# RG-LRU scan and gated causal convolution: the last root batch multiplied in channel order, and a new order of all queues

## The chip, the cores and the metric

The kernel runs on one core of a Trainium2 chip. Its engines work side by side, each through its own list of instructions in order: PE (matrix products and transposes, with the weight loads shown apart as PEld), DVE (VectorE), ACT (ScalarE), POOL (GpSimd) and SP, which here only issues the DMAs. The metric is the device time of one execution in microseconds. Before the change it is 291.31 us, the median of three runs (291.29, 291.31, 292.64).

## The reference

For inputs x, r_gate and i_gate of shape (4, 6336, 256), in float32, a gated linear recurrence runs over the 6336 steps of each of the four sequences, for 256 channels:

```python
log_a = c * sig_r * np.log(np.clip(a_base, 1e-06, 1.0 - 1e-06))[None, None, :]
a_t = np.exp(log_a)
norm = np.sqrt(np.maximum(1.0 - a_t * a_t, 1e-06))
x_gated = norm * sig_i * x
for t in range(S):
    h = a_t[:, t] * h + x_gated[:, t]
```

Here sig_r and sig_i are the sigmoids of the two gates and c is 8. The states h then go through a small network: a causal convolution of 5 taps per channel and a sigmoid give a gate, `h @ w_val` gives a value, and the output is `(gate * value) @ w_out`.

## The kernel before

The 25344 rows are cut into 51 windows: windows 0, 1 and 50 of 256 rows, all others of 512. One window or two make a chunk (28 chunks): chunks 0, 1 and 2 are windows 0, 1 and 2, chunks 3 to 25 have two windows each (chunk 25 is windows 47 and 48), and chunks 26 and 27 are windows 49 and 50. A window is loaded with rows on the 128 partitions; the recurrence needs channels there, in two halves h of 128 channels. So data is turned by transposes on PE, which write to PSUM (eight banks).

The steps have short names, and the number behind a name is a window or a chunk (and a half):

- `lr`, `li`, `lx` (SP, L279): loads of r_gate, i_gate and x for a window, into rings of four places each. `st` (SP, L507): store of the output, from a ring of four.
- `ta`, `tb` (ACT, L297, L300): tanh of half of r and i, the sigmoids in another form, for a chunk. The results are bfloat16; `tb` writes a ring of four places.
- `tr` (PE, L344) transposes `ta`'s result, `ex` (ACT, L360) takes the exponential: the coefficient a_t, channels on partitions, for a half of one chunk or of a pair of chunks.
- `sq` (POOL, L368) squares a_t into `ering`, for a chunk and half; `sa` (ACT, L376) does the same on ACT.
- `rt` (ACT, L393): the norm's square root of all the chunks of a root batch. There are eight batches, since root and exponential need different tables on ACT and each change costs a table load (L523). The last batch, `rt.7.0`, is chunks 25, 26 and 27.
- `pp` and `up` (POOL, L307, L319): gate of i plus one, and times x, into `uring`, with two rows interleaved as pairs of bfloat16 that pass through PE as one float32 word. For a few windows `xp` (PE, L324) and `uv` (DVE, L333) do this instead, with x copied to PSUM by a product with the identity.
- `nt` (PE, L407) transposes the norm back to rows on partitions, `xg` (DVE, L414) multiplies it into `uring`, in place.
- `xt` (PE, L422) transposes the product to channels, one bank for each half, and `sc` (DVE, L444) scans it together with a_t: this is the recurrence, with states in `yring`.
- `cv` (PE, L456): the convolution, 20 products of 64 by 64 weights for a window. `tg` (ACT, L463): its gate, a tanh. `vl` (PE, L471): the value. `gv` (DVE, L476): gate times value. `ou` (PE, L486): the output product. `cd` (DVE, L494) or `ca` (ACT, L496): the copy of it from PSUM for the store.

Nothing schedules these at run time. A string, ORDER, lists every step once, and the kernel emits them in that order (L518 to L524), so each engine's list is ORDER cut down to its own steps. What stands behind an @ are the banks of PSUM. An instruction that has to wait, for data, for a bank or for a place in a ring, holds up everything behind it on its engine.

## Time and profile before

| | |
|---|---|
| median of three runs | 291.31 us |
| the profiled execution | 293.39 us |
| span of the profile, first to last instruction | 291.6 us |
| mean granted clock of TensorE | 0.981 |
| read from HBM, written to HBM | 78.39 MB, 25.95 MB |

The profile is that of one execution. A row of groups tells line, engine, operation, the tiles written and read, the shapes, the count, and behind the bar the busy time in us, the mean of one instruction in ns, and the idle time of the engine just before, with what ended it. A row of the timeline has the start and the length in us in front; neighbours of one kind are merged (x2 is two instructions), and in brackets stands the idle time ahead of it.

### The profile page before, as it was taken

To read this page: it belongs to the slowest core of one execution; us is meant where nothing else is said; L and a number is where in the kernel's file an instruction comes from. 1 tells how busy PE (TensorE), PEld (TensorE's weight loads), DVE (VectorE), ACT (ScalarE), POOL (GpSimd) and SP (SyncE) were. 2 spreads that over 40 slices of the span, in tenths; PEclk is the share of its full clock that TensorE was granted. 3 is DMA by queue.
4 is the path that set the end of the run, shared out by engine and by line. 5 is a ranking of instruction groups with operands and counts; after the bars stand their busy time and mean duration, and the time that the engine had idled before them with its cause. 6 is when DMAs were issued, how large, how long until landed. Compare 5 with 4: busy or idle time off the path is not lost. (4 is left out here: it accounts for less than half of the span.)

```text
span 291.6 us, 6228 instructions
## 1 busy us (share of the span) xinstructions
PE 244.7 (84%) x2482; PEld 168.5 (58%) x2507; DVE 243.5 (83%) x201; ACT 272.4 (93%) x191; POOL 235.2 (81%) x156
## 2 busy tenths in 40 slices
...
GB/s 239 316 386 405 383 407 385 380 371 333 395 411 418 416 415 366 285 418 416 418 416 416 411 411 416 419 388 378 416 416 420 415 326 276 267 288 110 290 87 239
DMA packets 29995, 104.75 MB, mean 359 GB/s; under 512 B 3335, under 2 KB 3854, under 8 KB 29966
## 3 DMA queue, kind: packets, MB, share of 16 engines
...
q14 instruction: 10, 0.08, 0.1%
q10 hardware_dynamic: 14, 0.01, 0.0%
HBM read 78.39 MB, written 25.95 MB: 358 GB/s over the span
## 5 line engine op out<-in xcount | busy, mean ns | idle before, releaser
L444 DVE TENSOR_TENSOR_SCAN yring<-aring,yring,banks 128x1024 bf16<-128x1024 f32 (+5 forms) x54 | 106.8, 1993 | 2.6 <-PE banks L422 1.3
L368 POOL TENSOR_TENSOR ering<-aring 128x1024 f32<-128x1024 f32 (+2 forms) x55 | 92.6, 1709 | 16.4 <-ACT aring L360 16.3
L319 POOL TENSOR_TENSOR uring<-tbring,xring 128x1024 bf16<-128x1024 bf16 (+1 forms) x45 | 95.3, 2136 | 1.5 <-DMA xring<-in_x_dram 0.8
L476 DVE SCALAR_TENSOR_TENSOR tgring<-tgring,banks 128x1024 bf16<-128x1024 bf16 (+1 forms) x51 | 59.3, 1181 | 7.8 <-PE banks L471 2.8
L456 PE MATMUL banks<-yring,diag 64*64 64x512 bf16 (+7 forms) x1080 | 63.2, 365 | 1.4 <-DVE tgring L476 0.4
L307 POOL TENSOR_SCALAR tbring<-tbring 128x1024 bf16<-128x1024 bf16 (+1 forms) x45 | 46.2, 1039 | 14.9 <-ACT tbring L300 14.8
L486 PE MATMUL banks<-wo,tgring 128*128 128x256 bf16 x396 | 50.5, 273 | 8.9 <-DVE tgring L476 6.2
L463 ACT ACTIVATE tgring<-banks 128x1024 bf16<-128x1024 f32 (+1 forms) x51 | 50.2, 1007 | 4.2 <-PE banks L456 4.1
L360 ACT ACTIVATE aring<-banks,khf 128x2048 f32<-128x2048 bf16 (+3 forms) x34 | 53.4, 1610 | 0.7 <-POOL ering L368 0.3
L471 PE MATMUL banks<-yring,wv 128*128 128x512 bf16 (+7 forms) x191 | 48.4, 359 | 4.9 <-ACT aring L360 1.6
L486 PEld LDWEIGHTS <-tgring 128*128 128x128 bf16 x396 | 42.3, 114 | 17.5 <-DVE tgring L476 7.6
L297 ACT ACTIVATE taring<-rring 128x2048 bf16<-128x2048 f32 (+2 forms) x28 | 47.7, 1722 | 1.9 <-DMA rring<-in_r_gate_dram 1.9
L300 ACT ACTIVATE tbring<-iring 128x2048 bf16<-128x2048 f32 (+2 forms) x28 | 48.0, 1727 | 0.3 <-DVE uring L333 0.3
L456 PEld LDWEIGHTS <-diag 64*64 64x64 bf16 x1080 | 30.3, 107 | 25.2 <-issue 9.7
L393 ACT ACTIVATE ering<-ering 128x2048 bf16<-128x2048 f32 (+4 forms) x11 | 44.1, 4042 | 0.1
L344 PE MATMUL banks<-ident_b,taring 128*128 128x128 bf16 x396 | 29.9, 230 | 12.0 <-ACT taring L297 8.3
L494 DVE COPY oring<-banks 128x1024 f32<-128x1024 f32 (+1 forms) x31 | 36.3, 1182 | 3.6 <-PE banks L486 3.5
L422 PE MATMUL banks<-ident,uring 128*128 128x128 f32 x198 | 30.8, 283 | 7.8 <-DVE uring L414 4.4
L344 PEld LDWEIGHTS <-taring 128*128 128x128 bf16 x396 | 25.5, 103 | 17.6 <-ACT taring L297 10.2
L471 PEld LDWEIGHTS <-wv 128*128 128x128 bf16 x216 | 19.5, 97 | 23.4 <-issue 10.0
L414 DVE TENSOR_TENSOR uring<-banks,uring 128x2048 bf16<-128x2048 bf16 (+2 forms) x28 | 30.2, 1092 | 2.5 <-PE banks L407 2.1
L422 PEld LDWEIGHTS banks<-ident,uring 128*128 128x128 f32 x198 | 22.0, 142 | 16.3 <-DVE uring L414 7.6
...
## 6 DMA issues: line engine op xcount, KB each, us to landing
...
```

Of the source, the lines that this page charges most:

```text
L300: nc.scalar.activation(**tangent(c, tbring, NTI, iring, NII))
L319: nc.gpsimd.tensor_tensor(out=u, in0=t1, in1=xt, op=ALU.mult)
L344: nc.tensor.transpose(out=bank[:, o:o + P], in_=taring[:, place(w, NTR), j, h * P:(h + 1) * P], identity=ident_b[:])
L360: nc.scalar.activation(out=dst, in_=src, func=ACT.Exp, scale=khf[:, h:h + 1], bias=khf[:, h:h + 1])
L368: nc.gpsimd.tensor_tensor(out=e, in0=a, in1=a, op=ALU.mult)
L422: nc.tensor.transpose(out=bank[:, o + q:o + wins[w] // 2:nq], in_=uring[:, (w + 1) % NU, q, h * P:(h + 1) * P, :].rearrange("p d two -> p ...
L444: nc.vector.tensor_tensor_scan(out=yring[:, h, col:col + o1 - o0], data0=aring[:, h, a_at[c] + o0:a_at[c] + o1], data1=xT[:, o0:o1], initi ...
L456: nc.tensor.matmul(out=gp[oh * 64:oh * 64 + 64, h, a:b], lhsT=diag[half * 64:half * 64 + 64, h, k, :], rhs=yring[half * 64:half * 64 + 64, ...
L463: nc.scalar.activation(out=tgring[:, w % NTG, :, 0:wins[w]], in_=live.pop(("gp", w))[:, :, 0:wins[w]], func=ACT.Tanh, scale=0.5)
L471: nc.tensor.matmul(out=val[:, m, a:b], lhsT=wv[:, hk, m * P:(m + 1) * P], rhs=yring[:, hk, col:col + b - a], start=(hk == 0), stop=(hk == ...
L476: nc.vector.scalar_tensor_tensor(out=tgring[:, w % NTG, :, 0:wins[w]], in0=tgring[:, w % NTG, :, 0:wins[w]], scalar=1.0, in1=live.pop(("va ...
L486: nc.tensor.matmul(out=ops[:, j * D:(j + 1) * D], lhsT=gv[:, hk, j:wins[w]:J], rhs=wo[:, hk, :], start=(hk == 0), stop=(hk == H - 1))
```

## The change

The change has two parts.

First, chunks from 25 on (DIRECT), which are the last root batch, take another way to the scan. Before: root, `nt` (norm to rows), `xg` (product in rows, in place), `xt` (product to channels, in PSUM), `sc`. Now the gated input is transposed alone, both halves into one stretch of banks, and it does not wait for the root; `xg` multiplies it, read from PSUM, with the norm as it lies in `ering`, in channel order, and writes the product to `uring`; and `sc` reads its second operand there, in SBUF, where all other chunks read PSUM. `nt` is gone for these three chunks.

Second, ORDER is new from end to end. The counts of steps that differ: `nt` 28 to 25; windows gated by `xp` and `uv` 0, 1, 2, 8, 9, 18 to 1, 2, 7, 9, and so by `pp` and `up` 45 to 47; `sq` 55 to 53 and `sa` 1 to 3 (chunk 14's half 0 and chunk 27's half 1 move to ACT); copies `cd` 31 to 33 and `ca` 20 to 18. The start and the end of the two orders, and the code:

```diff
+DIRECT = 25
...
 ORDER = """
-s_ident s_small s_kt s_diag lr.0 lr.2 lr.1 li.0 lr.3 ta.0 ta.2 lr.4 tr.0.1@5 ta.1 tr.2.0@4 ex.0.1 lr.5 tr.1.1@0
-tr.2.1@7 ex.2.0 lr.6 sq.0.1 ex.1.1 li.2 ex.2.1 tr.0.0@0 tb.0 tr.1.0@7 ex.1.0 li.4 ex.0.0 lx.1 sq.1.0 ta.3 s_wl.3 sq.2.0
-lx.0 li.3 sq.0.0 lx.3 ta.4 sq.1.1 li.1 sq.2.1 lx.2 lr.8 tb.2 tr.3.1@0,1 ex.3.1 tr.3.0@6,7 li.6 lr.9 xp.0@3 lr.7 uv.0
-lx.4 ex.3.0 sq.3.1 s_wl.0 s_wl.2 tb.3 sq.4.1 lr.10 tb.1 xp.2@4,5 sq.3.0 xp.1@0 s_wl.1 uv.1 rt.0.0 li.8 sq.4.0 li.5 pp.3
-nt.0@6 rt.1.0 nt.1@7 lx.6 xg.1 pp.4 xg.0 xt.0.1@2 sc.0.1 up.3 uv.2 xt.1.1@2 xt.1.0@3 nt.2@6 xg.2 up.4 lx.7 sc.1.1 lx.5
-xt.2.0@7 ta.5 xt.0.0@0 xt.2.1@6 li.7 sc.0.0 nt.3@4,5 sc.1.0 s_wcast ta.6 xg.3 lr.11 cv.0@2,3 lr.12 sc.2.1 cv.1@4,5 tg.0
...
+s_ident s_small s_kt s_diag lr.0 lr.2 lr.1 lr.3 li.0 ta.0 ta.2 lr.4 ta.1 lr.6 tr.2.1@4 tr.0.1@0 lr.5 ex.2.1 tr.0.0@2
+tr.2.0@5 li.2 ex.0.1 lx.0 ex.2.0 tr.1.0@0 li.1 tr.1.1@3 tb.0 s_wl.0 ex.0.0 lx.1 pp.0 ex.1.0 li.3 ex.1.1 li.4 ta.3
+sq.1.1 sq.2.1 lx.2 sq.0.0 ta.4 lr.8 sq.2.0 s_wl.2 up.0 lr.7 tb.2 tr.3.1@2,3 lx.3 sq.1.0 lx.4 ex.3.1 sq.0.1 tr.3.0@6,7
+lr.9 tb.1 sq.4.1 s_wl.1 ex.3.0 li.6 sq.3.1 tb.3 xp.1@7 sq.3.0 li.7 uv.1 lr.10 rt.0.0 sq.4.0 xp.2@4,5 lx.6 uv.2 s_wl.3
+pp.4 nt.0@2 li.5 rt.1.0 xg.0 lx.5 pp.3 xt.0.0@7 xt.0.1@6 nt.2@1 li.8 xg.2 up.3 sc.0.1 xt.2.1@3 sc.0.0 nt.1@6 xt.2.0@0
+xg.1 up.4 lx.7 xt.1.1@1 xt.1.0@5 cv.0@6,7 sc.1.0 ta.5 sc.2.0 nt.3@4,5 tg.0 sc.1.1 s_wcast lr.11 ta.6 lr.12 xg.3
...
-tb.25 xg.24 xt.23.1@2 ou.40.0@6,7 sc.23.1 tg.41 pp.47 ou.39.0@0,1 ca.40.0 xt.24.0@5 sq.25.0 xt.24.1@4 ca.39.0 st.40
-tr.26.0@7 sc.24.0 lx.47 ex.26.0 vl.41@2,3 lx.50 cv.42@0,1 sa.26.1 st.39 sq.26.0 tb.27 st.38 cv.43@6,7 gv.41 tg.42
-sq.27.0 pp.49 sc.24.1 cv.44@2,3 tg.43 pp.48 pp.50 vl.42@0,1 up.48 gv.42 rt.7.0 ou.41.0@6,7 vl.43@4,5 cd.41.0 up.47
-ou.42.0@0,1 gv.43 st.41 cv.45@6,7 cd.42.0 up.49 nt.25@4,5 tg.45 xg.25 vl.45@0,1 tg.44 vl.44@6,7 gv.45 up.50 xt.25.1@5
-gv.44 ou.43.0@2,3 ca.43.0 ou.45.0@0,1 sc.25.1 xt.25.0@4 ca.45.0 st.43 ou.44.0@2,3 st.45 cv.46@6,7 ca.44.0 st.42 sc.25.0
-st.44 tg.46 vl.46@0,1 nt.26@2 nt.27@5 xg.26 cv.47@6,7 xg.27 gv.46 xt.26.1@5 tg.47 xt.26.0@4 sc.26.1 vl.47@2,3
-ou.46.0@0,1 sc.26.0 xt.27.1@5 ca.46.0 cv.48@6,7 gv.47 st.46 cv.49@0,1 tg.48 sc.27.1 tg.49 vl.48@2,3 xt.27.0@7 gv.48
-ou.47.0@4,5 ca.47.0 sc.27.0 vl.49@0,1 gv.49 st.47 ou.48.0@2,3 cv.50@4,5 ca.48.0 tg.50 ou.49.0@6,7 st.48 ca.49.0
-vl.50@2,3 gv.50 st.49 ou.50.0@4 ca.50.0 st.50
...
+tb.25 gv.41 vl.39@2,3 tr.25.0@7 xt.23.1@6 gv.39 ex.25.0 tr.26.0@1 pp.48 ou.40.0@4,5 sc.23.1 ex.26.0 pp.47 ou.39.0@2,3
+ca.40.0 xt.24.1@0 sq.25.0 xt.24.0@1 ca.39.0 st.40 cv.42@4,5 sc.24.0 tb.27 st.39 sq.26.0 sa.27.1 cv.43@6,7 lx.50 tg.42
+up.47 sc.24.1 tg.43 vl.43@2,3 ou.41.0@4,5 up.48 vl.42@6,7 cd.41.0 rt.7.0 cv.45@0,1 gv.43 st.41 pp.49 xt.25@4,5 gv.42
+cv.44@2,3 up.49 xg.25 ou.42.0@6,7 tg.44 sc.25.0 pp.50 vl.45@4,5 tg.45 up.50 ou.43.0@2,3 ca.42.0 cv.46@0,1 gv.45 ca.43.0
+st.42 sc.25.1 tg.46 vl.44@6,7 st.43 ou.45.0@2,3 xt.26@4 ca.45.0 xt.27@5 gv.44 cv.48@0,1 st.45 xg.26 cv.47@2,3 tg.48
+xg.27 sc.26.0 ou.44.0@4,5 sc.26.1 tg.47 vl.46@0,1 ca.44.0 gv.46 vl.48@6,7 vl.47@2,3 st.44 sc.27.1 gv.48 ou.46.0@0,1
+cv.49@4,5 ca.46.0 gv.47 st.46 tg.49 ou.48.0@6,7 sc.27.0 ca.48.0 vl.49@0,1 gv.49 st.48 ou.47.0@4,5 cv.50@2,3 cd.47.0
+tg.50 ou.49.0@6,7 st.47 ca.49.0 vl.50@0,1 gv.50 st.49 ou.50.0@3 ca.50.0 st.50
 """
...
         def op_xg(c):
+            u = u_of(c)
+            if c < DIRECT:
+                nc.vector.tensor_tensor(out=u, in0=live.pop(("nT", c)).bitcast(BF16), in1=u, op=ALU.mult)
+                return
+
+            o = 2 * live["n", c]
+            nc.vector.tensor_tensor(out=u, in0=live.pop(("uT", c)).bitcast(BF16),
+                                    in1=ering[:].bitcast(BF16)[:, o:o + H * clen[c]], op=ALU.mult)
+            for h in range(H):
+                live["xT", c, h] = u[:, h * clen[c]:(h + 1) * clen[c]]
...
+        def op_xt(c, *at):
+
+            if c < DIRECT:
+                h, b = at
+                words(c, h, banks[:, b])
+                live["xT", c, h] = banks[:, b].bitcast(BF16)
+                return
+            ps = banks[:, at[0]:at[-1] + 1].rearrange("p b n -> p (b n)")[:, 0:clen[c]]
+            for h in range(H):
+                words(c, h, ps[:, h * clen[c] // 2:(h + 1) * clen[c] // 2])
+            live["uT", c] = ps
...
         def op_sc(c, h):
-            xT = live.pop(("xT", c, h)).bitcast(BF16)
+            xT = live.pop(("xT", c, h))
```

Here `words` holds the transposes that stood in `op_xt`, and `u_of` the view of `uring` that stood in `op_xg`.

108 lines of the change are left out of this document (53 added, 55 removed).

## The prediction, made before the result was known

> **What bounds the kernel now.** I read the totals first, then the busy time by stretch of time, then the chain that ended last.
>
> ```profile
> span 291.6 us, 6228 instructions
> PE 244.7 (84%) x2482; PEld 168.5 (58%) x2507; DVE 243.5 (83%) x201; ACT 272.4 (93%) x191; POOL 235.2 (81%) x156
> ```
>
> ```profile
> 40.00:260.00 220.00, 196.57 (x2086) 136.46 (x2105) 207.60 (x159) 218.66 (x146) 205.29 (x126) 1.00 0.98 384
> 260.00:280.00 20.00, 19.84 (x200) 13.24 (x199) 19.45 (x18) 14.48 (x12) 8.55 (x6) 1.00 0.51 205
> 280.00:291.60 11.60, 6.56 (x64) 4.56 (x61) 4.24 (x5) 5.36 (x7) 0.00 (x0) 0.97 0.47 191
> 80.00:230.00 150.00, 133.96 (x1427) 92.73 (x1441) 141.71 (x111) 149.14 (x95) 146.41 (x88) 1.00 1.01 404
> ```
>
> The columns of a stretch are its length, then the busy us of PE, PE's weight loads, DVE, ACT and POOL. No engine stands out in the totals, but the stretches do: from 40 to 260 us ACT is busy 218.66 of 220.00, so there the time is ACT's list, instruction after instruction. From 80 to 230 POOL has only 3.59 us free as well. From 260 to 280 ACT has 5.5 us free, and PE (19.84 of 20) and DVE (19.45) carry the end. So there are three parts: a start in which ACT waits, a body that is ACT's with POOL close behind, and a tail that is PE's and DVE's.
>
> ```profile
> by line: PE banks L456 4.7%; PE banks L486 4.5%; PE banks L471 4.0%; PE banks L422 1.7%; PE banks L407 1.3%; PE banks L344 0.6%; DVE tgring L476 0.2%; ACT oring L496 0.2%; issue 0.2%; DVEq L476 0.0%; ACTq L496 0.0%
> ...
> 237.30 1.03 PE banks L486 x8
> ...
> 287.54 0.59 ACT oring L496
> ```
>
> The chain of waits says the same of the tail: back to 237.30 us it is all PE, and L407, the transposed norm that the change drops for three chunks, has 1.3% of the span in it.
>
> How close POOL stands to ACT is seen at the roots, which wait for POOL's squares:
>
> ```profile
> 142.06 1.90 POOL L368 TENSOR_TENSOR ering<-aring 128x1024 f32<-128x1024 f32 x1
> ...
> 144.10 7.04 ACT L393 ACTIVATE ering<-ering 128x8192 bf16<-128x8192 f32 x1
> ...
> 176.62 7.45 POOL L368 TENSOR_TENSOR ering<-aring 128x1024 f32<-128x1024 f32 x4
> ...
> 184.52 7.03 ACT L393 ACTIVATE ering<-ering 128x8192 bf16<-128x8192 f32 x1
> ```
>
> The last squares end 0.14 us before `rt.4.0` (142.06 + 1.90 against 144.10) and 0.45 us before `rt.5.0` (176.62 + 7.45 against 184.52). POOL work added ahead of these is no longer free after half a microsecond.
>
> **The work that changes hands.** Durations by shape (busy us, mean ns):
>
> ```profile
> L319 POOL TENSOR_TENSOR uring<-tbring,xring 128x1024 bf16<-128x1024 bf16 x44 | 94.2, 2158 | 1.5 <-DMA xring<-in_x_dram 0.8
> L444 DVE TENSOR_TENSOR_SCAN yring<-aring,yring,banks 128x1024 bf16<-128x1024 f32 x40 | 92.9, 2338 | 2.6 <-PE banks L422 1.3 <-PE banks L456 0.9 <-ACT aring L360 0.3
> L368 POOL TENSOR_TENSOR ering<-aring 128x1024 f32<-128x1024 f32 x46 | 86.0, 1896 | 6.7 <-ACT aring L360 6.7
> ...
> L307 POOL TENSOR_SCALAR tbring<-tbring 128x1024 bf16<-128x1024 bf16 x44 | 45.6, 1049 | 14.9 <-ACT tbring L300 14.8
> ...
> L494 DVE COPY oring<-banks 128x1024 f32<-128x1024 f32 x29 | 35.0, 1216 | 3.6 <-PE banks L486 3.5
> ...
> L496 ACT COPY oring<-banks 128x1024 f32<-128x1024 f32 x19 | 19.3, 1030 | 4.8 <-PE banks L486 4.8
> ...
> L444 DVE TENSOR_TENSOR_SCAN yring<-aring,yring,banks 128x512 bf16<-128x512 f32 x4 | 5.0, 1269 | 0.0
> ...
> L368 POOL TENSOR_TENSOR ering<-aring 128x256 f32<-128x256 f32 x6 | 3.6, 614 | 9.1 <-ACT aring L360 9.1
> ...
> L319 POOL TENSOR_TENSOR uring<-tbring,xring 128x512 bf16<-128x512 bf16 x1 | 1.2, 1178 | 0.0
> ...
> L376 ACT ACTIVATE ering<-aring 128x512 f32<-128x512 f32 x1 | 0.7, 727 | 0.0
> L307 POOL TENSOR_SCALAR tbring<-tbring 128x512 bf16<-128x512 bf16 x1 | 0.6, 621 | 0.0
> ```
>
> *ACT* loses two output copies (2 x 1.03) and gains two squares, one of 1024 elements, one of 256. No row has these. The long one lies between a copy of 1024 (1.03) and twice the row of 512 (1.45); the short one between 0.36 and 0.73. I take 1.15 and 0.5. That is -2.06 + 1.65 = **-0.4 us** on the list that sets the body (ends -0.7 and +0.1). Table loads: the same number.
>
> *POOL* gains the gating of window 0 (0.62 + 1.18) and, of the long windows, 8 and 18 for 7 (one pair, 1.05 + 2.16), and loses the two squares (1.90 + 0.61): +2.5 in all. Window 0 is gated in the start, when POOL waits for ACT (9.1 us idle ahead of its six short squares); I cost it at nothing, and 1.8 if that cover is gone.
>
> *The roots.* Counted over both orders between `rt.3.0` and `rt.5.0`, ACT has the same work except one copy that has become the long square (+0.1), while POOL's squares for `rt.5.0` come behind one more pp, one more up and one square less: 1.05 + 2.16 - 1.90 = +1.31. With the lead of 0.45 and ACT's +0.1, `rt.5.0` waits 1.31 - 0.45 - 0.1 = **+0.8 us**. Ends: 0, if POOL closes up its own free time (3.59 us between 80 and 230), and 1.8, if ACT also comes there 1 us earlier, as the next item says, and POOL does not. Between `rt.5.0` and `rt.6.1` both lists get shorter by about as much as each other, so I see no second wait.
>
> *The start.* ACT runs into one wait there:
>
> ```profile
> 31.11 1.33 DVE L333 SCALAR_TENSOR_TENSOR uring<-tbring,banks 128x512 bf16<-128x512 bf16 x2
> ...
> 32.80 3.71 ACT L297 ACTIVATE taring<-rring 128x2048 bf16<-128x2048 f32 x2
> ...
> 33.22 0.74 DVE L444 TENSOR_TENSOR_SCAN yring<-aring,yring,banks 128x256 bf16<-128x256 f32 x1
> ...
> 34.30 0.69 DVE L444 TENSOR_TENSOR_SCAN yring<-aring,banks 128x256 bf16<-128x256 f32 x1 [0.33 <-PE banks L422]
> 34.48 1.91 PE L407 MATMUL banks<-ident,ering 128*128 128x128 f32 x8
> ...
> 36.33 1.28 PE L456 MATMUL banks<-yring,diag 64*64 64x256 bf16 x20
> ...
> 37.66 0.60 ACT L463 ACTIVATE tgring<-banks 128x512 bf16<-128x512 f32 x1 [1.15 <-PE banks L456]
> ```
>
> The first gate of the convolution, `tg.0`, stood behind `ta.5` and `ta.6` and still waited 1.15 us. Its convolution, at 36.33, stood on PE behind the norm of chunk 3 (`nt.3`, 1.91 us), and the scan that it needs, at 34.30, on DVE behind `uv.2` (1.33) and a scan of chunk 1 (0.74). The new order puts `uv.2` ahead of the first norm, about where the first root ends and DVE is idle, `sc.0.0` ahead of chunk 1's scans and `cv.0` ahead of `nt.3`. So the scan can end 2.1 us sooner (34.30 + 0.69 - 2.07 = 32.9), and `cv.0`, with the two words of chunk 1 still before it, runs from about 33.5 to 34.8, while ACT comes to `tg.0` after one tanh at 32.80 + 1.86 = 34.7. The set of ACT instructions ahead of `rt.0.0` is the same, and so are the loads that they need. The wait shrinks to about 0.1: I take **-1.0 us**, if the body keeps it (ends -1.15 and 0).
>
> *The tail.* ACT has the same fifteen instructions after `rt.7.0` (7 gates, 8 copies), so its end, R, sets the place from which to count.
>
> ```profile
> 250.44 2.94 ACT L300 ACTIVATE tbring<-iring 128x1024 bf16<-128x1024 f32 x2
> ...
> 261.26 3.19 ACT L393 ACTIVATE ering<-ering 128x3584 bf16<-128x3584 f32 x1
> ...
> 264.77 1.23 PE L407 MATMUL banks<-ident,ering 128*128 128x128 f32 x8
> ...
> 266.11 1.23 DVE L414 TENSOR_TENSOR uring<-banks,uring 128x2048 bf16<-128x2048 bf16 x1 [0.35 <-PE banks L407]
> ...
> 282.42 0.74 DVE L444 TENSOR_TENSOR_SCAN yring<-aring,yring,banks 128x256 bf16<-128x256 f32 x1
> ...
> 283.83 0.74 PE L456 MATMUL banks<-yring,diag 64*64 64x256 bf16 x20
> ```
>
> Before, R = 261.26 + 3.19 = 264.45; the norm's eight transposes follow, and `xg.25` starts at 266.11, R + 1.66. Now the gated input is transposed ahead of R, and `xg.25` needs only the root and DVE, which stands behind `cd.41`, `gv.43`, `gv.42`: one copy (1.2) fewer than before since `sc.24.1`. So `xg.25` starts at about R + 0.1, 1.5 us sooner. From there to the end of `sc.27.0` DVE has the same instructions (five gv, three xg, six scans), 266.11 to 283.16, 17.0 us; PE has the six transposes of the last two norms fewer between, and the eight of `xt.25` done before. I let DVE keep its pace: `sc.27.0` ends 1.5 to 2.2 us sooner. But what then comes late is PE: `cv.50`, which before started 0.67 us after that scan, now stands behind `ou.46`, `cv.49`, `ou.48`, `vl.49` and `ou.47`, which wait in their turn for `gv.46` to `gv.47`. Walking this stretch by the durations above I get `cv.50` at 282.7 in place of 283.83; behind it the end is as before (one gate, one gv, one product, one copy, one store). **-1.1 us**. The ends are -2.2, if PE keeps up, and 0, if DVE comes to `xg.25` no sooner than before, so that the step taken off the path was not on it.
>
> This needs `up.47` and `up.48` before R, as `xt.25` reads them and stands on PE ahead of `cv.44`. POOL does pp.48, pp.47, two squares and these two ups after `tb.25` (before: 250.44 + 2.94 = 253.38): 2 x 1.05 + 1.9 + 1.0 + 2 x 2.16 = 9.3, so 262.7, and `xt.25` is through near 264.0, half a microsecond before R. If POOL is later, xt.25 holds up PE one for one.
>
> The scan of these chunks reads its second operand from SBUF. Its rate cannot be seen beforehand; the slope of the two rows (1.069 us for 512 elements) leaves 0.20 us of fixed time in a scan, so six scans could save between 0 and 1.2 us, or lose if SBUF is shared badly (below). I take 0, since nothing in the trace shows a SBUF form. [...]
>
> **Sum.** -0.4 + 0.8 - 1.0 - 1.1 = -1.7 us. The profiled execution took 293.39 us, 1.8 more than its span; its own sum is 291.7. The median of the three runs shown is 291.31, 2.1 below the profiled one, so I put the same difference on it: **289.6 us**, 0.6% faster. About 0.5% (1.46 us) is what a measurement of this kernel can tell from no change: below 289.85 is faster, above 292.77 slower.
>
> **Rivals.**
> - *The start's microsecond is not kept* (0.20). The next roots wait for squares anyway, and POOL is not earlier. -0.4 + 0.8 - 1.1 = -0.7: 290.6. For it: the leads of 0.14 and 0.45; against: POOL's idle time (14.8 us of the row of L307 above, all behind ACT's tanh) is waiting for ACT, so POOL would move up with it. In a quarter of this case I count the other way to 290.7: the start is kept, and the step dropped from the tail was not on the path (-1.7 + 1.1).
> - *POOL takes the place of ACT* (0.20), the slower case. If the free 3.59 us of POOL can't be used, its whole +2.5 lands ahead of the roots, and again at `up.48`, so that R, `xt.25` and PE behind it are late and the gains on ACT and in the tail are hidden: 291.3 + 2.5 = 293.8. It decides as soon as the last square of a batch ends after ACT has come to its root (0.14 us at `rt.4.0`), and in the tail as soon as `up.48` ends later than R - 1.2. For it: 146.41 of 150; against: only 0.7 of the 2.5 falls after the start.
> - *POOL closes up* (0.12): no wait at `rt.5.0`, -2.5: 288.8.
> - *The scan from SBUF quarrels with POOL* (0.08). `sc.25.0` and `sc.25.1` run while POOL still has pp and up of windows 49 and 50 (5.0 us). If each takes turns, half of the two scans (2 x 2.34 / 2 = 2.3 us) is added on DVE's path: 291.9. Against it:
>
> ```profile
> 261.05 7.50 POOL L319 TENSOR_TENSOR uring<-tbring,xring 128x1024 bf16<-128x1024 bf16 x4
> ...
> 269.51 4.58 DVE L444 TENSOR_TENSOR_SCAN yring<-aring,yring,banks 128x1024 bf16<-128x1024 f32 x2
> ```
>
> Scans with one operand in PSUM don't notice POOL now: after POOL's last instruction (268.55) two take 4.58 us, 2.3 each, against 2.34 in the mean. [...]
>
> **Chances.** The forecast has 0.40, with a spread of its own from 288.9 to 290.4, two thirds of it under 289.85. Faster: 0.27 + 0.12 + 0.03 of the lost start = 0.42. Within 0.5%: 0.13 + 0.17 + 0.05 + 0.01 = 0.36. Slower: 0.19 of POOL + 0.03 of the scan = 0.22. The range goes from 288.2 to 293.8, which leaves out half of POOL's case and the best of the closing up.
>
> **What would show it.** Start: no wait ahead of the first gate, and ACT busy from 32 us on. Roots: the last squares of `rt.5.0` end at ACT's arrival or later. ACT's busy total 272.0. Tail: no L407 after about 255 us, the direct xg starting within 0.3 us of R, and the last scan to the end in about 9 us. Scans of the last chunks at 2.34 us or less. The forecast is wrong if ACT shows waits of over 1 us between 40 and 260, on loads or on tbring, or if the transposes of the gated input wait for POOL after R.

## The result and the profile after

The changed kernel takes 289.62 us, the median of 15 runs (288.84 to 290.85). The kernel before takes 292.57 us in the 15 runs beside it (291.00 to 294.82). The ratio is 0.9901, with a 95% interval from 0.9877 to 0.9924: about 1% faster. The profiled execution took 289.94 us, 3.45 less than that of before (293.39), and 3.5 us of span are gone (288.1 against 291.6).

The totals of the page after, and the busy time by stretch:

```profile
span 288.1 us, 6219 instructions
PE 243.0 (84%) x2487; PEld 163.7 (57%) x2487; DVE 243.9 (85%) x200; ACT 271.5 (94%) x191; POOL 239.9 (83%) x158
```

```profile
40.00:260.00 220.00, 198.38 (x2095) 134.28 (x2093) 208.14 (x159) 218.38 (x145) 207.76 (x126) 1.00 0.99 388
260.00:280.00 20.00, 19.73 (x198) 12.55 (x194) 19.09 (x18) 14.78 (x14) 7.14 (x5) 1.00 0.40 159
280.00:288.10 8.10, 2.97 (x39) 1.97 (x36) 2.53 (x3) 2.19 (x3) 0.00 (x0) 0.93 0.57 228
80.00:230.00 150.00, 134.96 (x1438) 92.50 (x1437) 143.41 (x112) 148.50 (x91) 145.25 (x88) 1.00 1.02 407
```

The body looks as it did: ACT is busy 218.38 of 220 us (218.66 before), with POOL close behind. The totals don't tell where 3.5 us went; the ends of the program do. First the start, in the timeline of ACT (start, length; in brackets the wait ahead of it):

```profile
5.50 2.10 ACT L297 ACTIVATE taring<-rring 128x512 bf16<-128x512 f32 x3
...
13.90 1.91 ACT L297 ACTIVATE taring<-rring 128x2048 bf16<-128x2048 f32 x1 [0.55 <-DMA rring<-in_r_gate_dram]
...
24.57 5.60 ACT L393 ACTIVATE ering<-ering 128x2048 bf16<-128x2048 f32 x2
...
33.39 0.60 ACT L484 ACTIVATE tgring<-banks 128x512 bf16<-128x512 f32 x1
...
36.08 1.91 ACT L300 ACTIVATE tbring<-iring 128x2048 bf16<-128x2048 f32 x1 [0.29 <-DMA iring<-in_i_gate_dram]
...
38.37 4.00 ACT L360 ACTIVATE aring<-banks,khf 128x2048 f32<-128x2048 bf16 x2
```

The same place of the kernel before, where the prediction did not look:

```profile
5.44 2.10 ACT L297 ACTIVATE taring<-rring 128x512 bf16<-128x512 f32 x3
...
14.96 1.91 ACT L297 ACTIVATE taring<-rring 128x2048 bf16<-128x2048 f32 x1 [1.89 <-DMA rring<-in_r_gate_dram]
...
22.32 2.43 ACT L300 ACTIVATE tbring<-iring 128x2048 bf16<-128x2048 f32 x2 [0.32 <-DVE uring L333]
...
40.43 4.01 ACT L360 ACTIVATE aring<-banks,khf 128x2048 f32<-128x2048 bf16 x2
```

The wait at `tg.0` is gone, as forecast (33.39, no bracket). But so is most of a wait that was not in the forecast: `ta.4` waited 1.89 us for its load and now waits 0.55. The first root, from 26.07 to 24.57, comes 1.5 us sooner before `tg.0` has played any part. The last rows are `ex.5.1` and `ex.5.0`, the first exponentials behind `tg.0` and `tg.1`: the same ACT instructions stand ahead of them in both kernels.

The tail, in the timeline of all engines:

```profile
258.59 3.19 ACT L393 ACTIVATE ering<-ering 128x3584 bf16<-128x3584 f32 x1
...
261.34 2.16 POOL L319 TENSOR_TENSOR uring<-tbring,xring 128x1024 bf16<-128x1024 bf16 x1
...
261.94 1.22 DVE L422 TENSOR_TENSOR uring<-banks,ering 128x2048 bf16<-128x2048 bf16 x1
...
263.19 2.45 DVE L465 TENSOR_TENSOR_SCAN yring<-aring,yring,uring 128x1024 bf16<-128x1024 f32 x1
...
263.46 2.60 POOL L307 TENSOR_SCALAR tbring<-tbring 128x512 bf16<-128x512 bf16 x1
...
266.14 1.18 POOL L319 TENSOR_TENSOR uring<-tbring,xring 128x512 bf16<-128x512 bf16 x1
...
266.67 2.78 DVE L465 TENSOR_TENSOR_SCAN yring<-aring,yring,uring 128x1024 bf16<-128x1024 f32 x1
...
277.87 0.74 DVE L465 TENSOR_TENSOR_SCAN yring<-aring,yring,uring 128x256 bf16<-128x256 f32 x1
...
280.19 0.74 PE L477 MATMUL banks<-yring,diag 64*64 64x256 bf16 x20
...
283.91 0.59 ACT L517 COPY oring<-banks 128x512 f32<-128x512 f32 x1 [0.93 <-PE banks L507]
```

The last root ends at R = 258.59 + 3.19 = 261.78, and the direct `xg.25` starts at 261.94, R + 0.16 (before: R + 1.66). The last copy ends 22.7 us after R (before: 287.54 + 0.59 - 264.45 = 23.7). Two rows are new: the scans of chunk 25 take 2.45 and 2.78 us in place of 2.34, and `pp.50`, which took 0.62, takes 2.60.

One thing makes the profiles easier to compare. The first tanh starts between 4.74 and 5.51 us from one execution to the next, whatever the kernel. Below, times of the start and the body are counted from that tanh, and times of the tail from R. So counted, the last root starts at 255.8 before and at 253.1 after (-2.7), and from R to the last copy it is 23.7 and 22.7 (-1.0): two gains, one made in the start and kept through the body, one made in the tail.

### The profile page after: what moved, and what is told of

It is laid out like the page before. It is cut to its first block, busy times and chain, and to the rows that moved or that the text cites. A ratio compares the mean times of both kernels' runs of the same rounds, so it can differ in the third digit from the quotient of the medians.

```text
span 288.1 us, 6219 instructions
## 1 busy us (share of the span) xinstructions
PE 243.0 (84%) x2487; PEld 163.7 (57%) x2487; DVE 243.9 (85%) x200; ACT 271.5 (94%) x191; POOL 239.9 (83%) x158
## 4 chain that ended last, share of the span: by engine, by line
ACT 31%; PE 18%; issue 15%; DVE 14%; POOL 11%; DMA 9%; SPq 1%; ACTq 0%; DVEq 0%; POOLq 0%
ACT aring L360 7%; ACT tbring L300 6%; ACT taring L297 6%; ACT tgring L484 6%; DVE yring L465 5%; POOL ering L368 5%; DVE tgring L497 5%; POOL uring L319 4%; PE banks L477 4%; PE banks L492 4%; PE banks L507 4%; DMA xring<-in_x_dram 3%; DMA oring<-in_moe_w_out_dram 3%; DVE oring L515 2%; ACT oring L517 2%
## 5 line engine op out<-in xcount | busy, mean ns | idle before, releaser
L319 POOL TENSOR_TENSOR uring<-tbring,xring 128x1024 bf16<-128x1024 bf16 (+1 forms) x47 | 98.8, 2116 | 3.0 <-DMA xring<-in_x_dram 1.8
L465 DVE TENSOR_TENSOR_SCAN yring<-aring,yring,banks 128x1024 bf16<-128x1024 f32 (+5 forms) x48 | 97.9, 2058 | 1.3 <-PE banks L432 1.2
L368 POOL TENSOR_TENSOR ering<-aring 128x1024 f32<-128x1024 f32 (+2 forms) x53 | 90.3, 1728 | 3.9 <-ACT aring L360 3.3
L307 POOL TENSOR_SCALAR tbring<-tbring 128x1024 bf16<-128x1024 bf16 (+1 forms) x47 | 50.0, 1073 | 18.6 <-ACT tbring L300 18.5
L507 PE MATMUL banks<-wo,tgring 128*128 128x256 bf16 x396 | 51.2, 274 | 5.6 <-DVE tgring L497 3.6
L492 PE MATMUL banks<-yring,wv 128*128 128x512 bf16 (+4 forms) x216 | 50.0, 361 | 7.0 <-ACT tgring L484 2.5
L507 PEld LDWEIGHTS <-tgring 128*128 128x128 bf16 x396 | 41.6, 114 | 16.4 <-DVE tgring L497 8.6
L477 PEld LDWEIGHTS <-diag 64*64 64x64 bf16 x1080 | 28.8, 107 | 27.0 <-issue 10.9
L515 DVE COPY oring<-banks 128x1024 f32<-128x1024 f32 (+1 forms) x33 | 38.3, 1181 | 4.0 <-PE banks L507 3.8
L344 PEld LDWEIGHTS <-taring 128*128 128x128 bf16 x396 | 25.8, 104 | 15.2 <-ACT taring L297 9.8
L418 DVE TENSOR_TENSOR uring<-banks,uring 128x2048 bf16<-128x2048 bf16 (+2 forms) x25 | 27.9, 1131 | 4.7 <-PE banks L407 4.3
L432 PEld LDWEIGHTS banks<-ident,uring 128*128 128x128 f32 x198 | 22.2, 141 | 16.1 <-DVE uring L418 7.4
```

What stands on the lines that cost most here:

```text
L319: nc.gpsimd.tensor_tensor(out=u, in0=t1, in1=xt, op=ALU.mult)
L344: nc.tensor.transpose(out=bank[:, o:o + P], in_=taring[:, place(w, NTR), j, h * P:(h + 1) * P], identity=ident_b[:])
L368: nc.gpsimd.tensor_tensor(out=e, in0=a, in1=a, op=ALU.mult)
L465: nc.vector.tensor_tensor_scan(out=yring[:, h, col:col + o1 - o0], data0=aring[:, h, a_at[c] + o0:a_at[c] + o1], data1=xT[:, o0:o1], initi ...
L477: nc.tensor.matmul(out=gp[oh * 64:oh * 64 + 64, h, a:b], lhsT=diag[half * 64:half * 64 + 64, h, k, :], rhs=yring[half * 64:half * 64 + 64, ...
L492: nc.tensor.matmul(out=val[:, m, a:b], lhsT=wv[:, hk, m * P:(m + 1) * P], rhs=yring[:, hk, col:col + b - a], start=(hk == 0), stop=(hk == ...
```

## The experiments

The kernels, with what their profiles give. "Last root" is the start of `rt.7.0` counted from the first tanh, "last copy" and "end of span" are counted from R. Each ratio is to executions of before on the same chip at the same time, whose medians are 292.40 to 292.77.

| kernel | median us (lowest to highest) | ratio to before, 95% interval | last root | last copy | end of span |
|---|---|---|---|---|---|
| before | 292.57 (291.00 to 294.82) | | 255.8 | 23.7 | 27.2 |
| changed | 289.62 (288.84 to 290.85) | 0.9901 [0.9877, 0.9924] | 253.1 | 22.7 | 26.3 |
| e1_new_start | 291.69 (290.12 to 293.62) | 0.9971 [0.9937, 1.0005] | 253.2 | 23.7 | 27.3 |
| e2_old_start | 293.53 (290.90 to 294.80) | 1.0011 [0.9975, 1.0047] | 257.1 | 22.7 | 26.6 |
| e3_direct_alone | 293.19 (290.64 to 295.70) | 1.0000 [0.9968, 1.0032] | 257.1 | 23.2 | 27.3 |
| e4_old_end | 292.00 (290.87 to 295.01) | 0.9985 [0.9954, 1.0016] | 253.4 | 25.0 | 28.7 |
| e5_changed_again | 289.54 (288.87 to 291.56) | 0.9903 [0.9868, 0.9937] | 253.2 | 22.7 | 26.4 |
| e6_all_direct | 371.51 (367.95 to 371.61) | 1.2664 [1.2604, 1.2723] | | | |
| e7_old_loads | 289.76 (288.98 to 291.39) | 0.9904 [0.9869, 0.9938] | 253.8 | 22.7 | 26.0 |
| e8_tail | 290.66 (289.51 to 292.39) | 0.9947 [0.9921, 0.9973] | 254.8 | 21.8 | 27.0 |
| e9_old_cv0 | 293.58 (291.64 to 294.04) | 1.0016 [0.9985, 1.0046] | 257.6 | 22.7 | 26.4 |
| e10_no_late_pool | 289.82, one run | | 254.0 | 22.2 | 25.8 |
| e11_early_load | 289.23 (288.48 to 290.89) | 0.9877 [0.9832, 0.9923] | 253.3 | 22.7 | 26.3 |
| e12_load_and_tail | 290.18 (289.15 to 290.77) | 0.9909 [0.9878, 0.9940] | 252.6 | 21.9 | 26.6 |

The theory: the start gives most of the gain, the direct way and its order of the tail give the rest, and the body only carries it. The rivals: the new order of the body is what counts, or the direct way is.

**The start alone.** Before's kernel with the first words of the new order, up to `xg.3`; everything else in the old order, with the norm transposed.

```diff
 ORDER = """
-s_ident s_small s_kt s_diag lr.0 lr.2 lr.1 li.0 lr.3 ta.0 ta.2 lr.4 tr.0.1@5 ta.1 tr.2.0@4 ex.0.1 lr.5 tr.1.1@0
...
+s_ident s_small s_kt s_diag lr.0 lr.2 lr.1 lr.3 li.0 ta.0 ta.2 lr.4 ta.1 lr.6 tr.2.1@4 tr.0.1@0 lr.5 ex.2.1 tr.0.0@2
...
+xg.1 up.4 lx.7 xt.1.1@1 xt.1.0@5 cv.0@6,7 sc.1.0 ta.5 sc.2.0 nt.3@4,5 tg.0 sc.1.1 s_wcast lr.11 ta.6 lr.12 xg.3
```

> The kernel before with the new order up to xg.3 alone (loads, windows 0 and 2, the first convolution), the rest in the old order and with the old way to the scan. Theory S (most of the gain is made in the start: ACT's waits before 40 us, 2.3 us fewer in the profile after, and the saturated body carries them to the end): -2 to -2.5 us, a ratio of about 0.992 to 0.993. Rival B (the body is set by POOL's squares, so the start's gain is lost again and the body's new order makes it): no change, 0.999 to 1.001.

In the profile the last root starts at 253.2, as in the changed kernel, and the tail is that of before (23.7). So in this trace 2.6 of the 2.7 us ahead of R are there with the start alone, and little is left for the new order of the body. The median is less clear: 291.69 is 1.0 us below the 292.65 of before beside it, where 2 to 2.5 had been expected, and the interval of the ratio holds 1. The profiled execution took 290.99, and others up to 293.62.

**All but the start.** The changed kernel with the old order up to `tg.1`.

```diff
 ORDER = """
-s_ident s_small s_kt s_diag lr.0 lr.2 lr.1 lr.3 li.0 ta.0 ta.2 lr.4 ta.1 lr.6 tr.2.1@4 tr.0.1@0 lr.5 ex.2.1 tr.0.0@2
...
+s_ident s_small s_kt s_diag lr.0 lr.2 lr.1 li.0 lr.3 ta.0 ta.2 lr.4 tr.0.1@5 ta.1 tr.2.0@4 ex.0.1 lr.5 tr.1.1@0
...
+xt.2.0@7 ta.5 xt.0.0@0 xt.2.1@6 li.7 sc.0.0 nt.3@4,5 sc.1.0 s_wcast ta.6 xg.3 lr.11 cv.0@2,3 lr.12 sc.2.1 cv.1@4,5 tg.0
```

> The changed kernel with the old order up to tg.1, the rest new. Theory S: what is left is the tail's 1.0 us and ACT's 0.4 us, -0.7 to -1.4 us, 0.995 to 0.998. Rival B: as good as the changed kernel, 0.990 to 0.992.

The tail keeps its gain (22.7), and the whole is no faster than before (1.0011, where 0.995 to 0.998 had been expected). The seam costs something of its own, in ACT's timeline:

```profile
37.52 0.60 ACT L485 ACTIVATE tgring<-banks 128x512 bf16<-128x512 f32 x1 [1.60 <-PE banks L478]
...
47.51 1.02 ACT L485 ACTIVATE tgring<-banks 128x1024 bf16<-128x1024 f32 x1 [1.40 <-PE banks L478]
```

ACT waits 1.60 us at `tg.0` (1.15 in the kernel before) and 1.40 us at a later gate, where the kernel before does not wait. So this run shows that the start is needed, not what it is worth.

**The direct way alone.** Before's order, with the last batch multiplied in channel order.

```diff
-nt.25@4,5 nt.26@2 nt.27@5 xt.25.1@5 xt.25.0@4 xt.26.1@5 xt.26.0@4 xt.27.1@5 xt.27.0@7
+xt.25@4,5 xt.26@2 xt.27@5
```

(The new words stand in the places of the `nt`; `pp.49` and `pp.50` are moved behind `up.47` and `up.49`.)

> The kernel before with the direct way for chunks 25 to 27 and nothing else new but what it needs on POOL (pp.49 and pp.50 behind up.47 and up.49). Theory T (the root's step through PE was on the path): -0.3 to -1.1 us, 0.996 to 0.999, with xg.25 within 0.3 to 1.3 us of the root's end. Rival N (it was not, since DVE's queue and PE's products set the tail): 0 to +0.5 us.

It brings nothing: 1.0000. `xg.25` starts at R + 1.56, as late as before, since the transposes and DVE's copies ahead of it stand where they stood. The tail gets 0.5 us shorter, by the transposes that are gone, and the whole of it doesn't show in the median. The direct way needs its order to be worth the rest.

**The old end.** The changed kernel up to `tg.43`, then the old order, with the norm transposed.

```diff
-DIRECT = 25
...
-vl.43@2,3 ou.41.0@4,5 up.48 vl.42@6,7 cd.41.0 rt.7.0 cv.45@0,1 gv.43 st.41 pp.49 xt.25@4,5 gv.42 cv.44@2,3 up.49 xg.25
...
+pp.49 cv.44@2,3 pp.50 vl.42@0,1 up.48 gv.42 rt.7.0 ou.41.0@6,7 vl.43@4,5 cd.41.0 ou.42.0@0,1 gv.43 st.41 cv.45@6,7
+cd.42.0 up.49 nt.25@4,5 tg.45 xg.25
...
```

> The changed kernel up to tg.43, behind it the old end with the old way to the scan. Theory T: 0.7 to 1.2 us slower than the changed kernel, so -1.7 to -2.3 us against before, 0.992 to 0.994. Rival N: as the changed kernel, 0.990 to 0.991.

The last root comes as early as in the changed kernel (253.4), and the tail is 2.2 us longer than there (24.95 against 22.71), 1.3 longer than before's own. Again the seam costs something: ahead of R, DVE stands idle for PE, and so `xg.25` starts only at R + 3.02, 1.36 us later than before.

```profile
259.35 1.22 DVE L477 SCALAR_TENSOR_TENSOR tgring<-tgring,banks 128x1024 bf16<-128x1024 bf16 x1 [1.18 <-PE banks L472]
...
264.32 1.22 DVE L415 TENSOR_TENSOR uring<-banks,uring 128x2048 bf16<-128x2048 bf16 x1 [0.36 <-PE banks L408]
```

So the 2.2 us are not the price of the old end alone (0.7 to 1.2 had been expected). The sign is plain, the size is not.

**The changed kernel again**, on the chip of e6, e7 and e8.

> The changed kernel once more, as the measure for the runs beside it. If the whole is worth what its first runs gave: ratio to before 0.988 to 0.992, the profile 2.5 to 4 us shorter than the kernel before in the same place of the trace. If the first runs flattered it and the parts are all there is: 0.994 to 0.998. First root 1.0 to 1.5 us earlier than before, the scans of chunk 25 at 2.4 to 2.5 and 2.7 to 2.8 us, the POOL instruction pp.50 above 2 us.

0.9903, and every row in its place; the scans of chunk 25 take 2.43 and 2.77 us. The whole holds.

**All chunks in the direct way.** The scan that reads SBUF cost little in the tail. Here all chunks do it, in the middle of POOL's work.

```diff
-DIRECT = 25
+DIRECT = 0
 ORDER = """
-nt.5@4,5 xg.5 xt.5.1@0 xt.5.0@7
+xt.5@4,5 xg.5
```

(and so for each chunk from 0 to 24)

> The changed kernel with all chunks in the new way (DIRECT = 0), each transposing of the gated input where the norm was transposed, so that every scan has two operands in SBUF while POOL works. Theory of contention (pp.50 went from 0.62 to 2.60 us beside a scan, the scans from 2.34 to 2.45 and 2.78): the 1024-element scans have a mean of 2.45 us or more, pp well above its 1.05, POOL's busy time goes from 240 to over 270, the roots wait for its squares, and the kernel takes 300 to 325 us. Rival, that the two long rows in the tail were a matter of that place (the end of pp.50 wrongly placed): scans at 2.3, POOL at 240, and 288 to 290, with PE's busy time 20 us less.

It takes 371.5 us, a quarter more, far above the 325 at which I had put the upper end. The totals, the scans and POOL's three kinds of work, by form:

```profile
span 369.7 us, 5834 instructions
PE 251.6 (68%) x2303; PEld 156.1 (42%) x2303; DVE 297.8 (81%) x200; ACT 275.6 (75%) x191; POOL 320.4 (87%) x158
```

```profile
L462 DVE TENSOR_TENSOR_SCAN yring<-aring,yring,uring 128x1024 bf16<-128x1024 f32 x40 | 129.4, 3252 | 0.0
L316 POOL TENSOR_TENSOR uring<-tbring,xring 128x1024 bf16<-128x1024 bf16 x45 | 121.5, 2714 | 1.1
L365 POOL TENSOR_TENSOR ering<-aring 128x1024 f32<-128x1024 f32 x45 | 102.7, 2303 | 5.2 <-ACT aring L357 5.2
L304 POOL TENSOR_SCALAR tbring<-tbring 128x1024 bf16<-128x1024 bf16 x45 | 79.3, 1772 | 10.5 <-ACT tbring L297 10.5
```

A scan goes from 2.34 to 3.25 us, `up` from 2.16 to 2.71, a square from 1.90 to 2.30, `pp` from 1.05 to 1.77. POOL's busy time grows by 80.5 us (239.9 to 320.4) and the span by 81.6 (288.1 to 369.7), and ACT, with the same 191 instructions, is busy 75% of the span. The bound is now POOL and the scans together: POOL's 239.9 us of work and 117.0 us of scans (106.8 of 54 and 10.2 of the eight that open a sequence, in the kernel before) come to 357 of the 370, an estimate of what they need if they never overlap. How the two engines meet is seen in two timelines of the same stretch, DVE's and POOL's:

```profile
150.54 2.68 DVE L462 TENSOR_TENSOR_SCAN yring<-aring,yring,uring 128x1024 bf16<-128x1024 f32 x1
...
154.33 4.10 DVE L462 TENSOR_TENSOR_SCAN yring<-aring,yring,uring 128x1024 bf16<-128x1024 f32 x1
```

```profile
151.05 3.02 POOL L304 TENSOR_SCALAR tbring<-tbring 128x1024 bf16<-128x1024 bf16 x1
154.14 6.21 POOL L316 TENSOR_TENSOR uring<-tbring,xring 128x1024 bf16<-128x1024 bf16 x2
```

The `pp` of 151.05 begins while a scan runs, which ends at 153.22. It ends at 154.07, 0.85 after that, a little less than one `pp` (1.05): it did next to nothing until the scan was through. Then two `up` begin at 154.14, and a scan at 154.33, just behind. One `up` at its usual 2.16 ends at 156.30, and the scan ends at 158.43, 2.13 later, about one scan. Then the second `up` ends at 160.35, 1.92 later. So they don't slow each other; each waits for the other's whole instruction, and who began first goes first. It holds all through e6: 36 of the 40 long scans begin behind a POOL instruction that still runs, and each of them is longer than 2.34 us by the rest of that instruction less 0.19 to 0.20 us; the other four take 2.34 or 2.35. In the tail of the changed kernel it explains all three rows: `sc.25.0` began 0.31 us before `up.49` ended (263.50) and lost 0.11; `pp.50` began behind that scan and waited it out; `sc.25.1` began 0.65 us before `up.50` ended (267.32) and lost 0.44. The scan of 154.33 began 1.97 us before its `up` ended and lost 1.76. Each time the loss is the rest of POOL's instruction less 0.2 us.

**The tail without POOL.** The changed kernel without `pp` and `up` of windows 49 and 50: the gates of these two windows are left out, so chunks 26 and 27 are computed from what lay in the ring.

```diff
-pp.49 up.49 pp.50 up.50
```

> The changed kernel without POOL's last four instructions (pp and up of windows 49 and 50 are left out, so chunks 26 and 27 are computed from old contents of the ring). Theory of contention: with POOL silent the scans of chunk 25 take 2.34 us like the others in place of 2.45 and 2.78, and from the last root's end to the last copy it takes 0.3 to 0.6 us less than 22.71. Rival, that a scan with two operands in SBUF is slower by itself at 1024 elements: 2.45 or more still.

DVE's timeline has the scans of chunk 25 at the length of all others:

```profile
263.40 2.35 DVE L466 TENSOR_TENSOR_SCAN yring<-aring,yring,uring 128x1024 bf16<-128x1024 f32 x1
265.67 1.20 DVE L498 SCALAR_TENSOR_TENSOR tgring<-tgring,banks 128x1024 bf16<-128x1024 bf16 x1
266.78 2.35 DVE L466 TENSOR_TENSOR_SCAN yring<-aring,yring,uring 128x1024 bf16<-128x1024 f32 x1
```

The last copy comes 22.2 us after R, 0.5 sooner than with POOL. So 0.5 us is the price of the quarrel in the changed kernel (one execution, and both scans take 2.35 us in place of 2.45 and 2.78), and a scan from SBUF is by itself as long as one from PSUM (2.35 against 2.34).

**The loads.** The changed kernel with two pairs of loads in the old order.

```diff
-lr.0 lr.2 lr.1 lr.3 li.0 ta.0 ta.2 lr.4 ta.1 lr.6 tr.2.1@4 tr.0.1@0 lr.5
+lr.0 lr.2 lr.1 li.0 lr.3 ta.0 ta.2 lr.4 ta.1 lr.5 lr.6 tr.2.1@4 tr.0.1@0
```

> The changed kernel with the order of two pairs of r loads as before: the first i load ahead of the fourth r load, and lr.5 ahead of lr.6; nothing else is moved. Theory that the loads carry half of the start's gain: ta.4 waits for its load again by over 1 us, rt.1.0 starts 1.0 to 1.4 us later than in the changed kernel, and the end comes as much later, 290.6 to 291. Rival, that the wait only turns into another one at the first roots or is absorbed by the roots' waits for POOL: rt.1.0 or the end within 0.3 us of the changed kernel.

```profile
4.75 2.09 ACT L298 ACTIVATE taring<-rring 128x512 bf16<-128x512 f32 x3
...
14.02 1.91 ACT L298 ACTIVATE taring<-rring 128x2048 bf16<-128x2048 f32 x1 [1.40 <-DMA rring<-in_r_gate_dram]
```

`ta.4` starts 9.27 us after the first tanh, against 8.40 in the changed kernel (13.90 - 5.50) and 9.52 in the kernel before. It waits 1.40 us, against 0.55. The last root starts at 253.8, 0.6 to 0.7 later than in the two profiles of the changed kernel; 1.0 to 1.4 had been expected. How far one profile carries is seen from the others: with the new order of the loads `ta.4` starts 8.0 to 9.0 us after the first tanh in nine profiles (8.4 in the mean), with the old order 9.5 to 10.0 in three (before, e2 and e3; 9.8). So the order of the loads is worth about 1.4 us at `ta.4`, and the two pairs are a part of it, of uncertain size. The median (289.76 against 289.54) does not show it; with intervals of a third of a per cent on either side it could not.

**The first convolution.** The changed kernel with `cv.0` behind `nt.3`, and the scans and `uv.2` in the old order.

```diff
-uv.2 s_wl.3 pp.4 nt.0@2 li.5 rt.1.0 xg.0 lx.5 pp.3 xt.0.0@7 xt.0.1@6 nt.2@1 li.8 xg.2 up.3 sc.0.1 xt.2.1@3 sc.0.0
-nt.1@6 xt.2.0@0 xg.1 up.4 lx.7 xt.1.1@1 xt.1.0@5 cv.0@6,7 sc.1.0 ta.5 sc.2.0 nt.3@4,5 tg.0 sc.1.1
+s_wl.3 pp.4 nt.0@2 li.5 rt.1.0 xg.0 lx.5 pp.3 xt.0.0@7 xt.0.1@6 nt.2@1 li.8 up.3 sc.0.1 uv.2 xg.2 xt.2.1@3
+nt.1@6 xt.2.0@0 xg.1 xt.1.1@1 xt.1.0@5 sc.1.1 sc.0.0 up.4 lx.7 sc.1.0 ta.5 sc.2.0 nt.3@4,5 cv.0@6,7 tg.0
```

> The changed kernel with the first convolution where it was: cv.0 behind nt.3 on PE, uv.2 and xg.2 behind the first scan, the scan sc.0.0 behind sc.1.1 on DVE. Theory that this order is the larger part of the start's gain and that the body keeps it: ACT waits 1 us or more for PE at tg.0 again, and counted from the first tanh rt.2.0 and the last root come 1.0 to 1.5 us later than in the changed kernel (last root near 254.3 in place of 253.1), 290.5 to 291 in time. Rival, that the wait at tg.0 is absorbed by what follows (the li.5 load, POOL at the roots): last root within 0.4 us of the changed kernel.

```profile
31.40 1.91 ACT L298 ACTIVATE taring<-rring 128x2048 bf16<-128x2048 f32 x1
38.00 0.60 ACT L485 ACTIVATE tgring<-banks 128x512 bf16<-128x512 f32 x1 [4.69 <-PE banks L478]
```

The wait is back, and it is 4.69 us, not 1.15: in the new order only one tanh stands ahead of `tg.0`, so it can be reached at 33.31 and stands there until PE is through. The last root starts at 257.6, 4.5 us later, where 1.0 to 1.5 had been expected, and the kernel is as slow as before (293.58). About 0.6 of this was there ahead of the edit: `ta.4` starts at 9.00 in this execution, by its load, in place of 8.40. At `ex.5.1` ACT is 4.9 us behind the changed kernel, so 220 us of body take back no more than 0.4. The order of a few words near 35 us is worth as much as the whole change, and a wait of ACT there goes to the last root almost one for one.

PE's clock has a part in these waits, and the forecast did not count it. By stretch, before and then e9 (the number behind POOL's is the granted clock):

```profile
31.50:38.30 6.80, 5.84 (x51) 4.73 (x53) 5.53 (x9) 5.64 (x5) 4.59 (x6) 0.50 1.02 407
```

```profile
30.60:40.80 10.20, 7.81 (x68) 5.75 (x69) 6.73 (x9) 5.50 (x5) 4.50 (x6) 0.50 1.01 390
```

In the changed kernel the clock is at 0.50 from 30.9 to 34.3 only. The 20 products of `cv.0` take 1.28 us before and after, in such a stretch; the 20 of `cv.50`, of the same shape, take 0.74 at full clock. How much of the 4.69 us this makes was not measured, nor what sets the length of the stretch.

**One load earlier.** The changed kernel's own wait in the start is for `li.5`: 0.29 us in the profile above, 0.42 in e5, 0.18 in e7 and 2.03 in e8, whose start is the same. `li.5` stands on SP behind `li.7`, which waits for `tb.3`.

```diff
-li.6 sq.3.1 tb.3 xp.1@7 sq.3.0 li.7 uv.1 lr.10 rt.0.0 sq.4.0 xp.2@4,5 lx.6 uv.2 s_wl.3 pp.4 nt.0@2 li.5
+li.6 li.5 sq.3.1 tb.3 xp.1@7 sq.3.0 li.7 uv.1 lr.10 rt.0.0 sq.4.0 xp.2@4,5 lx.6 uv.2 s_wl.3 pp.4 nt.0@2
```

> The changed kernel with one load moved: li.5 is issued ahead of li.7, which stands on SP until tb.3 has read its place at about 23 us. Theory that the spread of the start is this load (ACT waited for it 0.29, 0.42, 0.18 and 2.03 us in four executions): no wait ahead of the tanh of chunk 4, rt.2.0 at 56.3 or earlier counted from the first tanh, the median 0.3 to 0.8 us below the changed kernel's, its highest time below 291. Rival, that another load behind it comes late in its place (li.7, lr.10, lx.6): a wait of the same size elsewhere, no difference.

The wait for the load is gone. Another of 0.46 us, for PE, stands at a gate at 43.34 in its place, and the last root is at 253.3, where it was. 289.23 is the lowest median of all, but its interval (0.9832 to 0.9923) holds the changed kernel's 0.9901: not told apart. The wait at 43.34 need not come from the edit. e4 and e10 have one at the same gate, `tg.2` (0.57 and 0.64 us); in these three PE's granted clock is at 0.5 for 6.8 us on end, from 29 or 30 us on, and `cv.1` takes 1.28 us. In the changed kernel, e5, e7, e8 and e12 no such stretch is longer than 3.4 us, and none of these waits at `tg.2`; `cv.1` takes 0.85 us in the changed kernel.

**PE's order in the tail.** `cv.50` starts 1.58 us after the scan that it needs (277.87 + 0.74 to 280.19), behind `ou.47`. Windows 47 and 48 are exchanged, so that `ou.47` frees its place for `tg.50` sooner, and `cv.50` and `vl.50` go ahead of two output products.

```diff
-xg.27 sc.26.0 ou.44.0@4,5 sc.26.1 tg.47 vl.46@0,1 ca.44.0 gv.46 vl.48@6,7 vl.47@2,3 st.44 sc.27.1 gv.48 ou.46.0@0,1
+xg.27 sc.26.0 ou.44.0@4,5 sc.26.1 tg.47 vl.46@0,1 ca.44.0 gv.46 vl.47@6,7 vl.48@2,3 st.44 sc.27.1 gv.47 ou.46.0@0,1
-cv.49@4,5 ca.46.0 gv.47 st.46 tg.49 ou.48.0@6,7 sc.27.0 ca.48.0 vl.49@0,1 gv.49 st.48 ou.47.0@4,5 cv.50@2,3 cd.47.0
-tg.50 ou.49.0@6,7 st.47 ca.49.0 vl.50@0,1 gv.50 st.49 ou.50.0@3 ca.50.0 st.50
+cv.49@4,5 ca.46.0 gv.48 st.46 tg.49 ou.47.0@6,7 sc.27.0 ca.47.0 vl.49@0,1 gv.49 st.47 cv.50@2,3 tg.50 vl.50@4,5 gv.50
+ou.48.0@6,7 ca.48.0 ou.49.0@0,1 st.48 cd.49.0 ou.50.0@2 st.49 ca.50.0 st.50
```

> The changed kernel with windows 47 and 48 exchanged in the tail and cv.50, vl.50 put on PE ahead of ou.48 and ou.49. Theory that the last stretch is PE's order (cv.50 starts 1.57 us after the scan that it needs, behind vl.49 and an ou): cv.50 starts within 0.7 us of the end of sc.27.0 and the last copy comes 0.5 to 0.9 us sooner counted from the last root, 289.0 in time. Rival, that the end is set by the last copies and stores, which are as many: within 0.2 us.

```profile
37.12 1.91 ACT L301 ACTIVATE tbring<-iring 128x2048 bf16<-128x2048 f32 x1 [2.03 <-DMA iring<-in_i_gate_dram]
```

```profile
280.46 1.94 DVE L498 SCALAR_TENSOR_TENSOR tgring<-tgring,banks 128x1024 bf16<-128x1024 bf16 x2 [0.88 <-PE banks L493]
283.35 1.23 DVE L516 COPY oring<-banks 128x1024 f32<-128x1024 f32 x1 [0.95 <-PE banks L508]
```

The mechanism holds and the gain doesn't. `cv.50` starts 0.70 us after its scan, and the last copy (283.35 + 1.23 = 284.58) ends 21.8 us after R, 0.9 sooner. But the end of the span is at 27.0, 0.7 later. From the last copy to the end it takes 5.2 us (289.8 - 284.58), against 3.6 in the changed kernel: three stores, two of them of 512 KB, now become ready within about a microsecond, where they had come one by one. From 284 to 288 us the DMAs move 258, 401, 395 and 256 GB/s, one us after the other, and the span ends at 289.8; in the changed kernel it is 406, 406 and 346 from 283 to 286, and the end is at 288.1. In both the end comes some 2 us after the last bytes. The late load of the same profile (2.03 us of wait) belongs to its start, not to this edit, but it shows what the body does with a delay: against e5, `tb.4` is 1.6 us late, and the last root (254.8 against 253.2) is too.

A second try, on top of the early load, puts `ou.48` behind `cv.50` again, ahead of `vl.50`, and spreads the copies:

```diff
-cv.50@2,3 tg.50 vl.50@4,5 gv.50 ou.48.0@6,7 ca.48.0 ou.49.0@0,1 st.48 cd.49.0 ou.50.0@2 st.49 ca.50.0 st.50
+cv.50@2,3 tg.50 ou.48.0@6,7 ca.48.0 vl.50@4,5 gv.50 st.48 ou.49.0@0,1 ca.49.0 st.49 ou.50.0@2 cd.50.0 st.50
```

> e11_early_load with the tail of e8_tail, but ou.48 behind cv.50 again and the copies of windows 49 and 50 on ACT and DVE, so that the last stores of 512 KB leave 0.5 us apart from one another and not together. Theory that the last stores ate what e8_tail gained: cv.50 still at 17.5 after the last root's end, the end of the span 25.6 to 26.1 us after the last root's end (26.3 in the changed kernel, 27.0 in e8_tail), together with the load 288.5 to 289.2. Rival, that the stores set the end by their sum whatever the order: 26.3 or later.

The last copy is early again (21.9), and the end of the span, at 26.6, is not: 4.7 us for the last stores. At 290.18 it is no faster than the changed kernel. The rival holds here, with one profile for each of the two tries: once the last copies come close together, the stores behind them set the end.

## Why the prediction came out as it did

The time was hit (289.6 against 289.62), the size of the change was not: -1.7 us forecast, -2.95 between the medians and -3.45 between the two profiled executions. The forecast took the median of three runs, 291.31, as the level; fifteen runs put it at 292.57. Two errors, of 1.25 us each, met: that the time was hit is luck. Step by step:

- **ACT's list, -0.4.** Right: the two squares took 1.08 and 0.45 us, so 2.06 went and 1.53 came, -0.5. ACT's busy total is 271.5 (272.0 forecast); the table loads around the roots are 14 of 1.28 us in both traces. That it shortens the body isn't seen: from `rt.2.0` to `rt.7.0`, where all these instructions stand, ACT took 198.5 us before and 196.5 after, and 1.9 of this is a tanh that now stands ahead of `rt.2.0`. ACT's waits in this stretch went from 0.5 to 1.3 us (0.66 at `ex.21.1` for PE, 0.45 at `ex.11.1` for POOL).
- **The root that waits for POOL, +0.8.** Wrong; it is 0. The last squares end 0.12 us before `rt.5.0`, by POOL's timeline and ACT's:

```profile
172.13 9.33 POOL L368 TENSOR_TENSOR ering<-aring 128x1024 f32<-128x1024 f32 x5
```

```profile
181.58 7.04 ACT L393 ACTIVATE ering<-ering 128x8192 bf16<-128x8192 f32 x1
```

  What I left at its lower end is what happened: POOL closed up its own free time. From 140 to 184 us it is busy 43.63 of 44.00 us, where it was 42.80 before. POOL had been idle behind ACT, and an ACT that is ahead lets it start sooner too; counting only the instructions of both lists misses that. 0.12 us is left at this root.
- **The start, -1.0.** Right in mechanism and in size, and only half of what the start gave. The wait of 1.15 us at `tg.0` is gone, and e9 shows how much hangs on it: from `ta.4` to `ex.5.1` ACT took 25.5 us before (14.96 to 40.43) and 24.5 after (13.90 to 38.37). What failed is the sentence "The set of ACT instructions ahead of `rt.0.0` is the same, and so are the loads that they need." The set is the same, their order is not, and so the sum has the loads at nothing: counted from the first tanh, `ta.4` starts 1.1 us sooner. The two pairs of loads that e7 puts back are a part of this; the others that moved in the same stretch were not taken apart. The wait of 1.89 us stood in ACT's timeline, and I read that timeline only from 30 us on. Ahead of the last root the change brings -2.7 in all: -1.1 to `ta.4`, -1.0 from there to `ex.5.1`, -0.6 in the body, all of it between `ex.5.1` and `rt.2.0`.
- **The tail, -1.1.** Right, in its size partly by luck: -1.0 to the last copy, -0.8 to the end of the span. `xg.25` starts at R + 0.16 (R + 0.1 forecast), and PE is what comes late next, as said: `cv.50` at R + 18.4 (18.25 forecast). But in e10, without POOL beside the scans, `cv.50` starts at R + 17.9 and the last copy comes 1.5 us sooner than before: the walk through PE was 0.4 too long, and the scans, put at nothing, cost 0.5. e3 shows that the direct way alone gives 0.5 of the 1.0 to the last copy and nothing to the end of the span; the new order of the end with the old way was not run.
- **The scan from SBUF, 0.** The rival's quarrel is real, in another form (whole instructions, not turns), and its price smaller: 0.5 us (e10) and not 2.3, since only three POOL instructions stand beside two scans here, and each of the two begins when little is left of POOL's (0.31 and 0.65 us). With every scan in SBUF it costs 80 us (e6). That six scans could save up to 1.2 us was an estimate of mine, from the 0.20 us that the slope of two rows left over. Nothing of it was seen: with POOL silent, scans of 1024, 512 and 256 elements take 2.35 (e10), 1.26 and 0.74 us (the changed kernel) from SBUF and 2.34, 1.27 and 0.74 from PSUM (before).
- **The body.** In the profiles it keeps what the start gives or loses, to the last root: e1 is 2.3 us ahead of before at `ex.5.1` and 2.6 at the last root, e9 is 4.9 and 4.5 behind the changed kernel, e8 1.6 behind e5 at `tb.4` and at the last root. There the rival that the start's microsecond is not kept falls.

One thing stays open. In the profiles the start of the new order gives before's kernel nearly the full gain ahead of R (e1: 253.2), which would be some 2.4 us; the medians show 1.0 (291.69 against 292.65 beside it). The runs of before, e1, e2, e3 and e4, which have the old order in one part at least, spread over 3.5 to 4.2 us each (one of e3, at 295.70, left out); those of the changed kernel, and of e5, e7, e8, e9, e11 and e12, which move only a few words in it, over 1.6 to 2.9. Part of this is seen in the traces. From `rt.2.0` to `rt.7.0` the new body took 196.2 to 196.6 us in ten profiles, whatever their start and end. The old body, which has one tanh of 1.9 us more in this stretch, took 198.5, 198.2 and 199.9 (before, e1, e3). In e3 ACT waits there for a load, and then for POOL's square:

```profile
86.79 1.91 ACT L298 ACTIVATE taring<-rring 128x2048 bf16<-128x2048 f32 x1 [0.64 <-DMA rring<-in_r_gate_dram]
...
90.64 2.06 ACT L361 ACTIVATE aring<-banks,khf 128x2048 f32<-128x2048 bf16 x1 [1.02 <-POOL ering L369]
```

So the new order of the body may well be worth something in executions in which the old one waits, and that would hide a part of e1's gain in its median; three profiles of the old body don't show how often. It isn't the only source of the spread: e2, which has the new body, spreads over 3.9 us, and in one and the same start the load of `li.5` is late by 0.18 to 2.03 us and PE's clock is at half for 3.4 or 6.8 us on end.
